# A depthwise convolution and two MLPs on one core: another order for the weight decoding, for the rounding passes and for the half-row copies

## The chip, the core and the metric

The program runs on one core of one Trainium2 chip. The metric is device time in microseconds (us), from the launch of the program to its end. The kernel before took 2457.29 us (median of three runs, 2455.79 to 2460.45).

## The reference

```python
# x (4, 4096, 192); weight (8, 7); w_in (192, 2048) and w_out (2048, 192), twice, both in float64
w = softmax(weight, axis=-1)                         # 7 taps for each of 8 heads of 24 channels
x = causal depthwise convolution of x with w         # 16384 tokens x 192 channels
h = x @ moe_w_in;   x = (h * cos(h)) @ moe_w_out     # first MLP
h = x @ moe2_w_in;  g = where(h > 0, h, exp(min(h, 0)) - 1)
out = g @ moe2_w_out                                 # second MLP
```

The results are float32. TensorE takes a rounded 32-bit type, so each operand is split into a high part and a low part (value minus high part), and each product is made of three: low x high, high x low, high x high.

## The kernel before

**Blocks, passes, steps.** The 16384 tokens are 32 blocks of 512. Four blocks make a group, and a group is done in two passes of 32 steps: first MLP (m = 1) for its four blocks, then second MLP (m = 2) for the same four. There are eight groups, so 512 steps, 8 to a block. A step handles two of the 16 slices of 128 hidden units.

**One step.** `emit_A(s)` issues 18 matmuls in 9 pairs into two PSUM tiles, `u` and `v` (192 channels are 128 + 64, so every product is cut into 64-row pieces that run in pairs). `emit_B(s - 2)` issues the 20 matmuls (10 pairs) of the second product for the step two earlier. Between them lie, for each of the two slices: `act1` (ScalarE, reads PSUM), for m = 1 also `mid` (VectorE), `act2` (ScalarE: Sin or Exp), `g` (VectorE, reads PSUM again and so frees it), then `emit_hi` (ScalarE rounds g to `gh`) and `emit_lo` (GpSimd subtracts: `gl`). `hi` and `lo` of step s are issued in step s + 1, and B uses them in step s + 2. In B, pairs 1 to 3 read `gh` of the first slice, 4 and 5 its `gl`, 6 to 8 `gh` of the second and 9 and 10 its `gl`.

**Order.** The order on every engine is the order in which `step` writes the instructions; engines run their own list in order and wait on semaphores. In a step of the kernel before, ScalarE has: act1 of both slices, then hi, act2, hi, act2.

**End of a block.** In the step with j = 1 of the next block `evac` copies two accumulators out (ScalarE, `e`, L574), adds the two others to them (VectorE, L577), and queues `sums`: a ScalarE copy of a half (L585), a GpSimd add (L587), and then for m = 1 the split of the result for the second MLP (ScalarE `zh`, `zc`, GpSimd `zl`, `zc`) or for m = 2 two VectorE transposes and six output DMAs. `sums` and the splits are generators in a list of chores; two chore calls are made in a step, the first in the list goes first.

**Operands of the next block.** `split` (m = 1) rounds the convolved block and fills the four doubled tiles `sh`, `sl`, `ch`, `cl` by eight half-row DMAs; `double_z` does so for m = 2. They are begun AHEAD steps before the block. All those DMAs, the x loads and the output go through SP's queue, which waits in order.

**Convolution.** The first four blocks are convolved with matrix products; later ones on VectorE (a transpose and seven passes, L347 to L360), two calls of the generator `cq` a step while m = 2 runs. When the convolution of a block begins, the x load of a later block is issued (`load_a`, L252).

**Weights.** They are float64 in DRAM and are decoded by integer operations, in 24 pieces of up to 256 columns for each MLP: part one (ScalarE 1 or 2, VectorE 3 or 4 instructions, L178 to L184), a GpSimd add (L186), a ScalarE rounding (L218, L239), a GpSimd subtraction (L220, L241). `prepare` keeps up to four pieces in flight and moves each one stage a call; `need` calls it until the weights of a step are there. The second MLP's raw pieces use three buffers and may start when block 3 is convolved.

Of the kernel before, what the change touches and what calls it, by code (L numbers as in the profile page):

```python
# [17 lines left out]
P = 128  # L18
N = 512
# [7 lines left out]
EARLY = 4  # L27
CALLS = 4
FLIGHT = 4
PRE1, PRE2 = 10, 3  # L30
W = 256
ROWS = 4
AHEAD = 5
# [4 lines left out]
def conv_then_two_mlps(ctx, tc, x, weight, w_in1, w_out1, w_in2, w_out2, out):  # L38
# [36 lines left out]
    stage = brief.enter_context(tc.tile_pool(name="stage", bufs=FLIGHT))  # L75
# [85 lines left out]

    def decode(m, load, n):

        raw = raw_tile(m)[:, 0:n]
        load(raw)
        yield  # L170
        lo, hi = raw[..., 0], raw[..., 1]
        w = stage.tile([P, W], F32, tag="w", name="w")[:, 0:n]
        bits = w.bitcast(I32)

        both = two if m == 1 else stage.tile([P, 2, W], F32, tag="t", name="t", bufs=1)
        size, low = both[:, 0, 0:n], both[:, 1, 0:n]
        if m == 1:
            nc.scalar.activation(out=size, in_=f32(hi), func=AF.Abs)  # L178
        else:
            nc.vector.tensor_scalar(out=size.bitcast(I32), in0=hi, scalar1=~SIGN, scalar2=0, op0=ALU.bitwise_and, op1=ALU.bitwise_or)  # L180
        nc.scalar.activation(out=low, in_=lo.bitcast(U32), func=AF.Copy, scale=2.0 ** -51, bias=2.0)
        nc.vector.tensor_scalar(out=size, in0=size, scalar1=2.0 ** -15, scalar2=2.0 ** 17 - 2.0 ** 13, op0=ALU.max, op1=ALU.min)
        nc.vector.tensor_scalar(out=bits, in0=size.bitcast(I32), scalar1=3, scalar2=0, op0=ALU.logical_shift_left, op1=ALU.bitwise_or)
        nc.vector.scalar_tensor_tensor(out=lo, in0=hi, scalar=SIGN, in1=low.bitcast(I32), op0=ALU.bitwise_and, op1=ALU.bitwise_or)  # L184
        yield
        nc.gpsimd.tensor_tensor(out=bits, in0=bits, in1=lo, op=ALU.add)  # L186
        yield w

    def prep_w_in(m, kind, j, n, queue):
# [29 lines left out]
        yield  # L219
# [3 lines left out]
    def prep_w_out(m, part, f0, f1, queue):  # L223
# [16 lines left out]
        yield  # L240
# [158 lines left out]
    def conv_by_products(what, b):  # L399


        xT = xTs.pop((what, b))
        if what == "a":
            o = ps_h.tile([P, N], F32, tag="u0", name="y")
        else:
            o = yb.pop() if yb else ps_a.tile([P, N], F32, tag=ACC[3], name="y")
        taps = lower_taps if what == "a" else upper_taps
        for k, w in enumerate(taps):
            nc.tensor.matmul(o, lhsT=w, rhs=xT[0:w.shape[0], k * Q:k * Q + N], start=k == 0, stop=k == len(taps) - 1)
            yield  # L410
        if what == "a" and b > 1:
# [25 lines left out]
    def doubles():  # L437
        return [dup.tile([P, N], F32R, tag=n, name=n) for n in ("sh", "sl", "ch", "cl")]
# [9 lines left out]
    def upper_split(b):  # L448

        yc = ys.pop(("c", b))  # L450
        ready_x[b] = d = doubles()
        nc.scalar.activation(out=d[2], in_=yc, func=AF.Copy)
        nc.vector.tensor_tensor(out=d[3], in0=yc, in1=f32(d[2]), op=ALU.subtract)

    def split(b):
        if ("c", b) in ys and b >= 2:
            yield from split_pair(b)
        ya = ys.pop(("a", b))
        xh = xt.tile([P, N], F32R, tag="xh", name="xh")
        xl = xt.tile([P, N], F32R, tag="xl", name="xl")  # L460
        nc.scalar.activation(out=xh, in_=ya, func=AF.Copy)
        yield
        nc.vector.tensor_tensor(out=xl, in0=ya, in1=f32(xh), op=ALU.subtract)
        split_done.add(b)
        yield
# [149 lines left out]
    def prepare():  # L615


        q = deque()
        for m in (1, 2):
            order = []  # L620
            for j in range(0, NP, 2):
                order += [("o", j, 1), ("c", j, 2), ("os", 2 * j, 4), ("oh", 2 * j, 2)]
                order += [("o", j + 1, 1), ("oh", 2 * j + 2, 2)]
            if m == 1:
                order[0:2] = [(0, 0, 1), (1, 0, 1), ("c", 0, 1), ("o", 1, 1), ("c", 1, 1)]
                order.remove(("o", 1, 1))
                order.insert(3, ("o", 1, 1))
            for kind, f0, n in order:
                queue = nc.scalar if len(q) < 2 else nc.sync
                if kind in ("os", "oh"):  # L630
                    g = prep_w_out(m, int(kind == "os"), f0, f0 + n, queue)
                else:
                    g = prep_w_in(m, kind, f0, n, queue)
                q.append(((kind, m, f0 + n), g))
        loaded, flight = deque(), deque()
        while len(loaded) < limit[1]:
            next(q[0][1])
            loaded.append(q.popleft())
        yield
        while q or loaded or flight:  # L640
            while q and len(loaded) + len(flight) < limit[q[0][0][1]] and (q[0][0][1] == 1 or ROWS - 1 in conved):
                next(q[0][1])
                loaded.append(q.popleft())
            if loaded and len(flight) < lanes[0]:
                flight.append(loaded.popleft())
            for it in list(flight):
                try:
                    next(it[1])
                except StopIteration:
                    flight.remove(it)  # L650
                    kind, m, at = it[0]
                    for k in ((0, 1) if kind == "o" else (kind,)):
                        ready[k, m] = at
            yield
        prepared.add(True)

    ready, prepared, banks = {}, set(), []
    limit, lanes = {1: PRE1, 2: PRE2}, [3]

    def need(m, at, *kinds):  # L660
        while any(ready.get((k, m), 0) < at for k in kinds):
            next(prep)

    prep = prepare()

    def convs():
# [10 lines left out]
        lower()  # L677
# [34 lines left out]
    begin_at = {max(s - AHEAD, 0): (m, b) for (m, b), s in first.items() if (m, b) != (1, 0)}  # L712
# [9 lines left out]
    def step(s):  # L722
# [11 lines left out]
        for q in now:  # L734
            emit_act1(q)
        for q in now:
            emit_mid(q)
# [4 lines left out]
        if 0 <= s - LAG < total:  # L742
# [3 lines left out]
            if j == NP - 1:  # L746
                finish = evac(m, b)
        for i in (0, 1):
            if calls > i:
                next(prep, None)  # L750
# [3 lines left out]
            if now:  # L754
                emit_act2(now[i])
            next(finish, None)
            if now:
                emit_g(now[i])
            busy = chore()
            if s < NP:  # L760
                for _ in range(EARLY // 2):
                    next(cq, None)
            elif len(conved) < GROUP or s >= total or steps[s][0] == 2:
                next(cq, None)
        for _ in range(calls - 2):
            next(prep, None)
# [8 lines left out]
    with tc.manual_schedule():  # L775
# [4 lines left out]
        next(prep)  # L780
# [4 lines left out]
        next(prep)  # L785
        next(prep)
        upper()
        n = 0
        while 0 not in conved:
            next(cq)  # L790
            n += 1
            if n in (5, 7, 9):
                next(prep)
        lanes[0] = FLIGHT
        for i, _ in enumerate(split(0)):
            if i == 1:
                upper_split(0)
# [33 lines left out]
```

## Time and profile before

| | |
|---|---|
| median of three runs | 2457.29 us |
| profiled execution: time / span | 2456.48 us / 2454.8 us |
| PE (matmul) busy | 2342.7 us, 95% |
| ScalarE, VectorE, GpSimd busy | 76%, 66%, 65% |
| mean granted TensorE clock | 0.982 |
| DMA | 112.14 MB, mean 46 GB/s |

The page's slices show PE at 99 to 100% from about the seventh slice on and lower before it: the first 300 us are another regime than the rest. PE is the engine that is nearest to its limit, so the question for every stretch is how much longer it is than the matmuls in it need, and which wait makes it so. A span of PE is modelled; where a stretch is measured below it is by the start times of the first matmul of B in a step.

### The profile page before, as it was taken

What the parts mean: (1) busy time and instruction counts of PE and PEld (TensorE: products, weight loads), DVE (VectorE), ACT (ScalarE), POOL (GpSimd) and SP (SyncE); (2) the same over time, 40 slices, a digit from 0 to 9 for tenths busy, and PEclk for the clock granted to TensorE, in tenths of its full rate; (3) what the DMA queues carried; (4) which work ended last, traced back from release to release, by engine and by line L of the source; (5) the groups of instructions that cost most, each with busy time, mean ns of one, the idle gap of its engine ahead of it and who ended that gap; (6) DMA issues with size and microseconds to landing.
All of it is one profiled execution on the core that took longest, in us unless ns stands there. A gap on an engine that the chain in (4) does not pass through costs nothing. (4 is left out here: it accounts for less than half of the span.)

```text
span 2454.8 us, 51057 instructions
## 1 busy us (share of the span) xinstructions
PE 2342.7 (95%) x19614; PEld 1896.1 (77%) x19614; DVE 1612.3 (66%) x2314; ACT 1860.3 (76%) x3544; POOL 1607.1 (65%) x1273
## 2 busy tenths in 40 slices
PE   7898699999999999999999999999999999999998
PEld 4576578887778877887877877788777887788886
DVE  5578687766756686666766667566776667666533
ACT  5576567887778877787777877778777887788876
POOL 5576656676666766576666676567666666667765
PEclk8999899999999999999999999999999999999999
DMA  5012223111311122212221212211132113112011
GB/s 152 18 40 69 67 51 71 34 44 30 60 37 36 36 55 41 54 29 48 43 47 38 53 30 53 43 42 36 36 60 46 26 36 60 31 42 53 19 36 26
DMA packets 279781, 112.14 MB, mean 46 GB/s; under 512 B 231920, under 2 KB 246512, under 8 KB 279536
## 3 DMA queue, kind: packets, MB, share of 16 engines
q1 hardware_dynamic: 279216, 108.62, 20.6%
q8 instruction: 153, 2.51, 0.4%
q14 instruction: 92, 0.75, 0.1%
q10 hardware_dynamic: 320, 0.26, 0.0%
HBM read 30.18 MB, written 12.58 MB: 17 GB/s over the span
## 5 line engine op out<-in xcount | busy, mean ns | idle before, releaser
L551 POOL TENSOR_TENSOR gl<-w,gh 128x512 fp32r<-128x512 f32 x1024 | 1359.1, 1340 | 797.5 <-ACT gh L546 481.4
L546 ACT ACTIVATE gh<-w 128x512 fp32r<-128x512 f32 x1024 | 645.9, 631 | 11.7 <-DVE w L540 8.0
L566 PE MATMUL b<-gh,wo_hl 64*128 64x512 f32 x2048 | 636.2, 391 | 10.4 <-DVE e L577 10.4
L566 PE MATMUL a<-gh,wo_hl 64*128 64x512 f32 x2048 | 638.8, 391 | 5.5 <-ACT gh L546 5.5
L566 PE MATMUL a<-gl,wo_hl 64*128 64x512 f32 x1024 | 409.1, 399 | 20.8 <-POOL gl L551 19.7
L540 DVE SCALAR_TENSOR_TENSOR w<-w,u 128x512 f32<-128x512 f32 x256 | 175.5, 686 | 381.5 <-ACT w L532 378.5
L566 PEld LDWEIGHTS a<-gh,wo_hl 64*128 64x128 f32 x2048 | 381.2, 186 | 57.6 <-ACT gh L546 6.0
L566 PEld LDWEIGHTS b<-gh,wo_hl 64*128 64x128 f32 x2048 | 379.4, 186 | 40.7 <-DVE e L577 18.5
L507 PE MATMUL u<-ch,wi_c 64*128 64x512 f32 x1024 | 401.9, 392 | 6.5 <-DMA ch<-ch 5.3
L566 PE MATMUL b<-gl,wo_hl 64*128 64x512 f32 x1024 | 406.3, 397 | 0.0
L507 PE MATMUL u<-sh,wi_o 64*128 64x512 f32 x1024 | 401.4, 392 | 1.6 <-DMA sh<-xh 1.6
L507 PE MATMUL v<-ch,wi_c 64*128 64x512 f32 x1024 | 400.9, 392 | 1.8 <-DMA ch<-ch 1.1
L507 PE MATMUL v<-sh,wi_o 64*128 64x512 f32 x1024 | 401.3, 392 | 0.0
L566 PE MATMUL b<-gh,wo_s 64*128 64x512 f32 x1024 | 400.0, 391 | 0.0
L566 PE MATMUL a<-gh,wo_s 64*128 64x512 f32 x1024 | 398.4, 389 | 0.0
L566 PE MATMUL a<-gl,wo_s 64*128 64x512 f32 x1024 | 397.8, 388 | 0.0
L566 PE MATMUL b<-gl,wo_s 64*128 64x512 f32 x1024 | 397.4, 388 | 0.0
L517 ACT ACTIVATE w<-u 128x512 f32<-128x512 f32 x256 | 152.6, 596 | 249.5 <-PE v L507 116.8
L515 ACT ACTIVATE w<-u 128x512 int32<-128x512 f32 x256 | 152.5, 596 | 235.0 <-PE v L507 94.4
L530 ACT ACTIVATE w<-w 128x512 f32<-128x512 f32 x512 | 321.6, 628 | 5.1 <-DVE w L524 4.9
L532 ACT ACTIVATE w<-w 128x512 f32<-128x512 f32 x512 | 321.9, 629 | 0.1
L524 DVE SCALAR_TENSOR_TENSOR w<-u,w 128x512 f32<-128x512 f32 x256 | 176.6, 690 | 217.3 <-ACT w L515 217.1
(128 smaller groups left out, 7117.6 us busy)
## 6 DMA issues: line engine op xcount, KB each, us to landing
out_dram<-e SPq DMA_DIRECT2D x192, 64.0 KB, 1.9
xa<-in_x_dram SPq DMA_DIRECT2D x112, 88.0 KB, 2.7
sh<-xh SPq DMA_DIRECT2D x64, 128.0 KB, 2.3
sl<-xl SPq DMA_DIRECT2D x64, 128.0 KB, 2.3
sh<-zh SPq DMA_DIRECT2D x64, 128.0 KB, 2.4
sl<-zl SPq DMA_DIRECT2D x64, 128.0 KB, 2.3
ch<-zc SPq DMA_DIRECT2D x64, 128.0 KB, 2.3
cl<-zc SPq DMA_DIRECT2D x64, 128.0 KB, 2.3
```

What stands on the lines that cost most here:

```text
L507: nc.tensor.matmul(u[i], lhsT=at, rhs=x[k + h][p], start=n == 0, stop=n == len(ops) - 1)
L515: nc.scalar.activation(out=w.bitcast(I32), in_=u, func=AF.Copy, bias=0.25)
L517: nc.scalar.activation(out=w, in_=u, func=AF.Relu, scale=-1.0)
L524: nc.vector.scalar_tensor_tensor(out=w, in0=u, scalar=0.25, in1=w.bitcast(I32), op0=ALU.add, op1=ALU.subtract)
L530: nc.scalar.activation(out=w, in_=w, func=AF.Sin, scale=6.283185)
L532: nc.scalar.activation(out=w, in_=w, func=AF.Exp, scale=-1.0)
L540: nc.vector.scalar_tensor_tensor(out=w, in0=w, scalar=-1.0, in1=u, op0=ALU.add, op1=ALU.max)
L546: nc.scalar.activation(out=gh, in_=wrk[s], func=AF.Copy)
L551: nc.gpsimd.tensor_tensor(out=gl, in0=wrk.pop(s), in1=f32(gs[s][0]), op=ALU.subtract)
L566: nc.tensor.matmul(a[o + i], lhsT=w[p, f, :], rhs=g[p], start=first, stop=final)
```

## The change

It has four parts.

- *Weight decoding.* `prepare` becomes `fetch` and `advance`. One call of `advance` does the rounding and subtraction of the piece before last, the add of the last one, and part one of a new piece. Three calls a step instead of four while the first MLP's weights are decoded, one a step afterwards. The order of pieces changes (`in_order`), a piece that was decoded twice is decoded once, and every second piece of the first MLP makes its absolute value on VectorE instead of ScalarE. The convolution's generator gets five calls a step until four blocks are convolved (before: four in the first eight steps, then two).
- *Rounding.* `hi` of the first slice comes first in a step, `hi` of the second in the middle. For m = 1: hi, act1, act1, hi, act2, act2; for m = 2: hi, act1, act2, hi, act1, act2. All of `evac` stands in the first half of a step.
- *Copies.* In `split`, each copy is issued right behind its source, `ch` and `cl` first.
- *AHEAD* is 6 instead of 5; block 1's convolved rows are copied from PSUM to SBUF; `lower()` is moved ahead of the first step.

```diff
-EARLY = 4
-CALLS = 4
-FLIGHT = 4
-PRE1, PRE2 = 10, 3
+EARLY = 5
+CALLS = 3
+RAW1, RAW2 = 10, 3
-AHEAD = 5
+AHEAD = 6
...
-        if m == 1:
+        turn[0] += 1
+        if m == 1 and turn[0] % 2:
             nc.scalar.activation(out=size, in_=f32(hi), func=AF.Abs)
...
     def split(b):
         if ("c", b) in ys and b >= 2:
             yield from split_pair(b)
+        sh, sl, ch, cl = doubles(("sh", "sl")) + ready_x.pop(b) if b < 2 else doubles()
+        if b >= 2:
+            p = half[b % 2]
+            both_halves(ch, pair["h"][p])
+            both_halves(cl, pair["l"][p])
...
         nc.scalar.activation(out=xh, in_=ya, func=AF.Copy)
+        swap(sh, xh)
         yield
         nc.vector.tensor_tensor(out=xl, in0=ya, in1=f32(xh), op=ALU.subtract)
+        swap(sl, xl)
         split_done.add(b)
-        yield
-        sh, sl, ch, cl = ready_x.pop(b) if b < 2 else doubles()
-        swap(sh, xh)
-        swap(sl, xl)
-        if b >= 2:
-            p = half[b % 2]
-            both_halves(ch, pair["h"][p])
-            both_halves(cl, pair["l"][p])
...
+    def fetch():
+        while todo and len(loaded) + len(begun) < raws[todo[0][1]] and (todo[0][1] == 1 or ROWS - 1 in conved):
+            next(todo[0][3])
+            loaded.append(todo.popleft())
+
+    def advance(new=True):
+        if added:
+            kind, m, at, g = added.popleft()
+            next(g)
+            for k in ((0, 1) if kind == "o" else (kind,)):
+                ready[k, m] = at
+        if begun:
+            next(begun[0][3])
+            added.append(begun.popleft())
+        if new and loaded:
+            next(loaded[0][3])
+            begun.append(loaded.popleft())
+        fetch()
...
-        for q in now:
-            emit_act1(q)
-        for q in now:
-            emit_mid(q)
...
+        first_mlp = now and steps[s][0] == 1
         for i in (0, 1):
-            if calls > i:
-                next(prep, None)
             if old:
                 emit_hi(old[i])
                 emit_lo(old[i])
-            if now:
+            if first_mlp and i == 0:
+                for q in now:
+                    emit_act1(q)
+                    emit_mid(q)
+            elif now and not first_mlp:
+                emit_act1(now[i])
                 emit_act2(now[i])
-            next(finish, None)
-            if now:
                 emit_g(now[i])
-            busy = chore()
-            if s < NP:
-                for _ in range(EARLY // 2):
-                    next(cq, None)
-            elif len(conved) < GROUP or s >= total or steps[s][0] == 2:
+            for _ in finish:
+                pass
+            if calls > i:
+                advance()
+            if first_mlp and i == 1:
+                for q in now:
+                    emit_act2(q)
+                    emit_g(q)
+            chore()
+            if len(conved) >= GROUP and (s >= total or steps[s][0] == 2):
                 next(cq, None)
```

In the order of the built programs (line numbers differ by one or two between them) this shows as follows. First ScalarE at a block's end in the first MLP, before:

```order
L546 ACTIVATE gh<-w 128x512
L530 ACTIVATE w<-w 128x512
L574 ACTIVATE e<-a_6108 128x512
L574 ACTIVATE e<-a_6110 128x512
L546 ACTIVATE gh<-w 128x512
L530 ACTIVATE w<-w 128x512
L585 ACTIVATE e<-e 64x512
L515 ACTIVATE w<-u 128x512
```

The same place now:

```order
L545 ACTIVATE gh<-w 128x512
L514 ACTIVATE w<-u 128x512
L514 ACTIVATE w<-v 128x512
L573 ACTIVATE e<-a_6096 128x512
L573 ACTIVATE e<-a_6098 128x512
L584 ACTIVATE e<-e 64x512
L545 ACTIVATE gh<-w 128x512
L529 ACTIVATE w<-w 128x512 x2
```

The copy of a half (L585, now L584), which stood behind the second rounding of `gh`, now stands ahead of it.

Next SP's queue where a second-MLP pass ends and the next group's first block gets its operands, before:

```order
L605 DMA out_dram<-e 32x16x32 x6
L252 DMA xa<-in_x_dram 32x22x32 x4
L442 DMA sh<-xh 64x512 x2
L442 DMA sl<-xl 64x512 x2
L446 DMA ch<-ch 64x512 x2
L446 DMA cl<-cl 64x512 x2
```

And now:

```order
L604 DMA out_dram<-e 32x16x32 x6
L446 DMA ch<-ch 64x512 x2
L446 DMA cl<-cl 64x512 x2
L442 DMA sh<-xh 64x512 x2
L442 DMA sl<-xl 64x512 x2
L252 DMA xa<-in_x_dram 32x22x32 x4
```

The x load, which was ahead of the eight copies, is behind them, and the `c` copies come first.

Last GpSimd in the first pass of group 0, where pieces of the second MLP's weights (adds L186, subtractions L220 and L241) stand among the `gl` of the steps, before:

```order
L241 TENSOR_TENSOR wo_hl<-w,wo_hl 128x256
L551 TENSOR_TENSOR gl<-w,gh 128x512 x2
L186 TENSOR_TENSOR w<-w,raw 128x256
L551 TENSOR_TENSOR gl<-w,gh 128x512 x2
L186 TENSOR_TENSOR w<-w,raw 128x256
L551 TENSOR_TENSOR gl<-w,gh 128x512 x2
L220 TENSOR_TENSOR wi_o<-w,wi_o 128x256
L186 TENSOR_TENSOR w<-w,raw 128x256
```

And now:

```order
L550 TENSOR_TENSOR gl<-w,gh 128x512 x2
L221 TENSOR_TENSOR wi_o<-w,wi_o 128x256
L188 TENSOR_TENSOR w<-w,raw 128x256
L550 TENSOR_TENSOR gl<-w,gh 128x512 x2
L221 TENSOR_TENSOR wi_o<-w,wi_o 128x256
L188 TENSOR_TENSOR w<-w,raw 128x256
L550 TENSOR_TENSOR gl<-w,gh 128x512 x2
L221 TENSOR_TENSOR wi_c<-w,wi_c 128x256
```

Before, 14 of the 24 pieces are added up to step 33 and the other ten in steps 34 to 39; now one piece is added in every step from 10 to 33, and it stands between the two `gl` of its step.

## Rows read from the trace of the kernel before

**Rows 1.** Page, part 1: busy us (share of the span) xinstructions of each engine.
```profile
PE 2342.7 (95%) x19614; PEld 1896.1 (77%) x19614; DVE 1612.3 (66%) x2314; ACT 1860.3 (76%) x3544; POOL 1607.1 (65%) x1273
```

**Rows 2.** B's matmuls (L566, 20 a step) by stretch: length, busy (count), clock, DMA.
```profile
46.70:126.00 79.30, 21.21 (x160) 0.91 0.11 30
126.00:255.20 129.20, 65.88 (x480) 0.97 0.20 53
255.20:319.20 64.00, 22.61 (x160) 0.84 0.28 65
...
434.50:574.30 139.80, 80.06 (x640) 1.00 0.15 34
574.30:725.00 150.70, 86.06 (x640) 0.98 0.25 49
```

**Rows 3.** The same, for eight steps each of passes of the second MLP.
```profile
1444.50:1482.30 37.80, 20.80 (x160) 1.00 0.24 48
1482.30:1518.80 36.50, 21.62 (x160) 1.00 0.32 61
...
1555.40:1595.20 39.80, 21.08 (x160) 0.96 0.24 47
2137.00:2171.80 34.80, 20.00 (x160) 1.00 0.20 43
```

**Rows 4.** Timeline of TensorE, SP's queue and ScalarE (start us, us): a group's first block.
```profile
1581.43 0.50 PE L507 MATMUL u<-ch,wi_c 64*128 64x512 f32 x1 [0.92 <-DMA ch<-ch]
...
1573.48 2.00 SPq L252 DMA_DIRECT2D xa<-in_x_dram  x4
...
1579.08 1.24 SPq L446 DMA_DIRECT2D ch<-ch  x2
...
1568.32 0.62 ACT L461 ACTIVATE xh<-y 128x512 fp32r<-128x512 f32 x1
```

**Rows 5.** Waits of 255.2 to 319.2 us: who for whom, total us, times, longest.
```profile
PE u L507 <- POOL wi_o L220: 18.8, 3, 10.1
```

**Rows 6.** Timeline of TensorE, ScalarE, VectorE, GpSimd: a block's end, first MLP.
```profile
1630.11 0.39 PE L566 MATMUL a<-gh,wo_hl 64*128 64x512 f32 x1
...
1631.92 0.39 PE L566 MATMUL a<-gl,wo_hl 64*128 64x512 f32 x1
...
1628.07 1.09 ACT L574 ACTIVATE e<-a 128x512 f32<-128x512 f32 x2
1629.03 0.65 ACT L546 ACTIVATE gh<-w 128x512 fp32r<-128x512 f32 x1
...
1630.22 0.63 ACT L585 ACTIVATE e<-e 64x512 f32<-64x512 f32 x1
1630.76 0.58 ACT L515 ACTIVATE w<-u 128x512 int32<-128x512 f32 x1
...
1628.82 1.28 DVE L577 SCALAR_TENSOR_TENSOR e<-b,e 128x512 f32<-128x512 f32 x2
...
1629.81 1.30 POOL L551 TENSOR_TENSOR gl<-w,gh 128x512 fp32r<-128x512 f32 x1 [0.72 <-ACT gh L546]
```

**Rows 7.** A piece of weights: VectorE and GpSimd timeline; GpSimd groups (busy, mean ns).
```profile
198.36 0.29 DVE L180 TENSOR_SCALAR t<-raw 128x256 int32<-128x256 int32 x1 [5.77 <-DMA raw<-in_moe_w_in_dram]
...
186.51 1.27 DVE L182 TENSOR_SCALAR t<-t 128x256 f32<-128x256 f32 x1
...
186.27 2.66 POOL L551 TENSOR_TENSOR gl<-w,gh 128x512 fp32r<-128x512 f32 x2
...
L186 POOL TENSOR_TENSOR w<-w,raw 128x256 int32<-128x256 int32 x24 | 19.0, 791 | 8.0 <-DVE raw L184 7.9
...
L241 POOL TENSOR_TENSOR wo_hl<-w,wo_hl 128x256 fp32r<-128x256 f32 x8 | 6.0, 756 | 0.0
```

**Rows 8.** VectorE and GpSimd timeline: a convolution pass beside three `gl`.
```profile
945.58 4.29 DVE L360 SCALAR_TENSOR_TENSOR y<-xT,wch,y 128x512 f32<-128x512 f32 x1
...
945.56 3.76 POOL L551 TENSOR_TENSOR gl<-w,gh 128x512 fp32r<-128x512 f32 x3
```

More of the change, by code (lines that the diff above doesn't have):

```diff
@@ L160, in raw_tile @@
         return t.rearrange("p (n two) -> p n two", two=2)
+    turn = [0]
     def decode(m, load, n):
@@ L410, in conv_by_products @@
             yield
-        if what == "a" and b > 1:
+        if what == "a":
             y = y_tile(what, b)
@@ L435, in conv_then_two_mlps, with doubles @@
     ready_x = {}
-    def doubles():
-        return [dup.tile([P, N], F32R, tag=n, name=n) for n in ("sh", "sl", "ch", "cl")]
+    def doubles(tags=("sh", "sl", "ch", "cl")):
+        return [dup.tile([P, N], F32R, tag=n, name=n) for n in tags]
     def swap(out, own):
@@ L450, in upper_split @@
         yc = ys.pop(("c", b))
-        ready_x[b] = d = doubles()
-        nc.scalar.activation(out=d[2], in_=yc, func=AF.Copy)
-        nc.vector.tensor_tensor(out=d[3], in0=yc, in1=f32(d[2]), op=ALU.subtract)
+        ready_x[b] = d = doubles(("ch", "cl"))
+        nc.scalar.activation(out=d[0], in_=yc, func=AF.Copy)
+        nc.vector.tensor_tensor(out=d[1], in0=yc, in1=f32(d[0]), op=ALU.subtract)
     def split(b):
@@ L612, in sums, with in_order @@
         yield
-    def prepare():
-        q = deque()
-        for m in (1, 2):
[L620 to L629, printed above, removed]
+    def in_order(m):
+        order = []
+        for j in range(0, NP, 2):
+            order += [("o", j, 1), ("c", j, 2), ("os", 2 * (j - 2), 4), ("oh", 2 * (j - 2), 2)]
+            order += [("o", j + 1, 1), ("oh", 2 * (j - 1), 2)]
+        order += [("os", NF - 4, 4), ("oh", NF - 4, 2), ("oh", NF - 2, 2)]
+        order = [o for o in order if o[1] >= 0]
+        if m == 1:
+            order[0:3] = [(0, 0, 1), (1, 0, 1), ("c", 0, 1), ("o", 1, 1), ("c", 1, 1)]
+        return order
@@ L630, in prepare, with pieces @@
+    def pieces():
+        for m in (1, 2):
+            for n, (kind, f0, c) in enumerate(in_order(m)):
+                queue = nc.scalar if m == 1 and n < 2 else nc.sync
                 if kind in ("os", "oh"):
-                    g = prep_w_out(m, int(kind == "os"), f0, f0 + n, queue)
+                    g = prep_w_out(m, int(kind == "os"), f0, f0 + c, queue)
                 else:
-                    g = prep_w_in(m, kind, f0, n, queue)
-                q.append(((kind, m, f0 + n), g))
@@ L635, in prepare @@
[L635 to L654, printed above, removed]
@@ L655, in prepare @@
-        prepared.add(True)
+                    g = prep_w_in(m, kind, f0, c, queue)
+                yield kind, m, f0 + c, g
+    todo = deque(pieces())
+    loaded, begun, added = deque(), deque(), deque()
+    raws = {1: RAW1, 2: RAW2}
+    def fetch():
[15 more added lines that the diff above has]
+        fetch()
+        if not (todo or loaded or begun or added):
+            prepared.add(True)
@@ L711, in conv_then_two_mlps @@
             first[m, b] = s
-    begin_at = {max(s - AHEAD, 0): (m, b) for (m, b), s in first.items() if (m, b) != (1, 0)}
+    begin_at = {max(s - AHEAD, EARLY): (m, b) for (m, b), s in first.items() if (m, b) != (1, 0)}
     chores = deque()
@@ L753, in step @@
                 emit_lo(old[i])
-            if now:
+            if first_mlp and i == 0:
[4 more added lines that the diff above has]
+                emit_act1(now[i])
                 emit_act2(now[i])
-            next(finish, None)
-            if now:
                 emit_g(now[i])
-            busy = chore()
-            if s < NP:
-                for _ in range(EARLY // 2):
-                    next(cq, None)
-            elif len(conved) < GROUP or s >= total or steps[s][0] == 2:
+            for _ in finish:
+                pass
+            if calls > i:
+                advance()
+            if first_mlp and i == 1:
[4 more added lines that the diff above has]
+            if len(conved) >= GROUP and (s >= total or steps[s][0] == 2):
                 next(cq, None)
         for _ in range(calls - 2):
-            next(prep, None)
+            advance()
+        if len(conved) < GROUP:
+            for _ in range(EARLY):
+                next(cq, None)
         if prepared and NP * GROUP <= s < 2 * NP * GROUP:
@@ L779, in conv_then_two_mlps @@
         load_pair(0, "ol")
-        next(prep)
+        fetch()
         nc.scalar.activation(out=spark, in_=ident[:, 0:H], func=AF.Exp)
@@ L784, in conv_then_two_mlps @@
         softmax_weights()
-        next(prep)
-        next(prep)
+        advance()
+        advance()
         upper()
@@ L791, in conv_then_two_mlps @@
             n += 1
[L792 to L797, printed above, removed]
+            if n in (6, 8):
+                advance(n == 6)
+        upper_split(0)
+        for _ in split(0):
+            pass
+        advance()
+        lower()
         need(1, 1, 0, 1, "c")
```

8 lines of the change are left out of this document (1 added, 7 removed).

## Prediction

> **What bounds the kernel now.** I read the page first, then B's matmuls by stretch, then the waits and the timelines where a stretch is too long. PE is busy for 95% of the span [rows 1], so what can be won or lost is the time by which a stretch exceeds its matmuls. Eight pairs of B take from 1630.11 to 1631.92 [rows 6], 0.226 us a pair; a step has 19 pairs, so 4.31 us. Against this [rows 2, 3]: a pass of 32 steps needs 137.9 us; first-MLP passes take 139.8 (2 us over), second-MLP passes 150.7 (13 over). In group 0, eight steps (34.5) take 79.3 at the start, 24 steps (103.4) take 129.2, and eight steps take 64.0 where the second MLP begins. Inside a second-MLP pass the quarters take 37.8, 36.5, about the same again, and 39.8: over by 3.3, 2.0, 2.0 and 5.3.
>
> The sum is made against the profiled execution, 2456.5 us (span 2454.8 and 1.7 around it); the median of the runs shown is 0.8 higher, so I add 0.8 at the end.
>
> **a) Copies with their source.** In the last quarter PE waits for `ch` [rows 4]: xh was made at 1568.3, but SP first waited to issue the x load (1573.48), then `sh` and `sl`, and `ch` only at 1579.08; PE got it at 1581.43. A last quarter in which no x load follows (the pass before the last group) takes 34.8 [rows 3]: 5.0 less, the halved clock after the wait included (0.96 against 1.00). In the new order the copies stand ahead of the x load, `ch` first, and are begun about a step and a half earlier; at most eight issues of 0.62 are ahead of any of them, so the last lands before the 8.6 us of two steps are over. Five crossings at 5.0, and the first group's, in the stretch before 434.5, at half of that: **-27 us**. Bounds: 0 if the copies stay late, -30.
>
> **b) Second MLP's weights.** In 255 to 319 us PE waits 18.8 us for GpSimd's `wi_o` pieces in three waits [rows 5], and starts anew at a low clock (0.84). Now the last piece is done by step 33. What stays is the change of pass (3.3 over, as in rows 3) and the convolution, which starts earlier by the same reason (I take 3): 34.5 + 6.5 = 41 for 64.0: **-23**. Bounds -28 (neither stays) and -15.
>
> **c) The same pieces inside the first pass.** Before, 14 pieces stand in these 24 steps, 25.8 us over, one wait of VectorE for a late raw piece (5.77, rows 7) among it. Now it is 24 pieces, one in each step, and the order closes a loop: `hi` of the first slice now precedes act1 on ScalarE, and needs g; g stands on VectorE behind part one of the piece; part one has to get past GpSimd. Alone, part one's passes take 0.29 each; beside a `gl` one took 1.27, until that `gl` ended [rows 7]. GpSimd's work in that place is `gl` 1.30 [rows 6], subtraction 0.76, add 0.79, `gl` 1.30: 4.1 us, begun 0.7 after g's end (`hi`, 0.65). Then two of part one's passes (0.29 and about 0.4) and g (0.64, as in the two of 1.28, rows 6): 0.7 + 4.1 + 0.7 + 0.64 = 6.2 a step; 6.85 if all four passes come after the last `gl`. I take 6.5, nearer to the row of 1.27: 24 x 6.5 + 3 for block ends = 159 for 129.2: **+30**. Bounds: without any waiting between the two engines the loop is `hi` and act1 (1.2), two mids (1.2), part one (1.3) and g (0.64), 4.4, so 24 x 4.4 + 6 = 112, -17; with all of it 24 x 6.85 + 6 = 170, +41.
>
> The Trainium skill has a rule for this, "SBUF — State Buffer", section "Who interferes with whom": a VectorE instruction with two SBUF inputs, or in a two-port mode, and a GpSimd instruction that reads SBUF exclude each other for a whole instruction, whoever issues first. The 1.27 beside 0.29 agrees. By it no VectorE pass waits for more than one GpSimd instruction, 1.3 us; but one convolution pass took 4.29 beside three `gl` of 3.76 together [rows 8], so the trace does not hold to that. With the rule at its word, the term e below would be 7 less.
>
> **d) First steps.** Up to 126 us no engine is full: VectorE, ScalarE and GpSimd each work little over half the time in a stretch of 79.3 for eight steps. The three stages no longer wait for one another inside a call, one piece of 25 is no longer done twice, and B of step 0 needs fewer pieces. From above, the engines' own work: GpSimd three pieces of 1.55 and two `gl`, 7.2 a step, 58 in all: -21. From below, VectorE's part one of the third piece and the convolution calls may now stand ahead of the next mid: +6. The nearest row is the 79.3 itself; I take a third of the way, **-8**. The copy of block 1, the earlier `lower()` and the absolute values moved to VectorE are in this.
>
> **e) Block ends.** Here the new order costs. At a block's end ScalarE copies two accumulators at 1628.07, VectorE adds from 1628.82 to 1630.10, and the copy of a half follows at 1630.22 [rows 6]. Before, the second `hi` (1629.03) was ahead of it, and its `gl` ended at 1631.1, in time for pair 9 of B at 1631.92. Now `hi` comes behind the copy, at 1630.76, ends at 1631.40, its `gl` runs to 1632.8: PE waits 0.95. Behind that, GpSimd's list in a first-MLP pass has eight operations of 1.26 in a row (gl, add, gl, gl, zl, gl, zc, gl); the last is now needed before it is done, by about 0.45. So 1.4 an end and 0.95 at the first end of a pass: 3 x 1.4 + 0.95 = 5.2 over, for 2.0 now. As the slots are tight I take 5.6: 7 passes (groups 1 to 7) x 3.6 = **+25**. Bounds +13 (first wait alone) and +42 (PE waits again for g).
>
> In second-MLP passes the quarters are now over by 3.3, 2.0, 2.0 and (without a) 0.3, 7.6 together. The first wait of 0.95 comes here too. Then, in two of the four ends, a convolution pass is pending on VectorE while GpSimd has gl, add, gl, gl; it gets in after one (second wait 0.95) or after three [rows 8] (2.2). I take 2.5 for each end, 3.4 for the change of pass, 1.0 for the last: 9.4, +1.8 x 6 passes, less 2 as their starts have more slack, and +2 in group 7, which has no convolution: **+11**. Bounds -7 and +24.
>
> Within a block nothing changes: ScalarE's passes follow each other by about 0.5 us [rows 6], six take 3.1 of 4.31 in either order, and the earlier `gl` only adds slack. That cover is gone at block ends alone, which is e.
>
> **Sum.** 2456.5 - 27 - 23 + 30 - 8 + 25 + 11 = 2464.5; with 0.8, **2465 us**.
>
> **Rivals.**
> *The pipeline pays (faster).* If part one slips between GpSimd's operations, the steps with a piece cost about 5.7, c is +10, and d comes out at the engines' own work, -21: 2465 - 20 - 13 = 2432. For it: VectorE passes of 0.29 are short, and the first MLP's pieces work in PSUM. Against it: the 1.27 row, and the loop over `hi`. It decides from a step of about 6.0 downwards.
> *GpSimd starves VectorE (much slower).* If passes wait for three operations as in rows 8 wherever GpSimd has a queue, c is +41, and e +42 and +24: 2465 + 11 + 17 + 13 = 2506. For it: the new order gives GpSimd longer queues at block ends. Against: of the convolution passes only a few at block ends show it.
> *The copies stay late.* If something else in SP's queue (raw pieces, outputs) is ahead, a is 0: 2492. Against it stands the order itself.
>
> **Chances.** My forecast 0.45 (its own range 2453 to 2480), pipeline pays 0.34, starving 0.16, copies late 0.05. The two large cases of both signs give 2425 to 2500 for 8 in 10. About 0.2% is what a measurement of this kernel can tell from no change, here 2452 to 2462; the forecast's lower edge and the pipeline case's upper one put 0.14 there, 0.38 below it and 0.48 above.
>
> **What would show it.** Right: no wait of PE for `ch` at the groups' crossings; PE without the 10 us waits at the second MLP's start; B of steps 8 to 32 in about 159 us; at each block end ScalarE's `gh` about 1.7 us later than now and PE waiting for `gl` about 1 us; first-MLP passes near 143.5 us, second-MLP passes near 147 to 148. Wrong: first-MLP passes still at 139.8 (then the half copy does not hold `gh` back in time that matters), steps with a piece below 6 us, or the start to 126 us shortened by more than 15.

## The result, and the profile after

The changed kernel takes 2473.7 us (median of four runs, 2472.95 to 2475.08) where the kernel before, run beside it, takes 2458.87 (2455.79 to 2462.28): a ratio of 1.0061, 95% interval 1.0043 to 1.0078. It is slower by 15 us, 0.4 to 0.8%. The forecast was 2465, slower by 8, with 2425 to 2500 as its range. In the profiled execution the span is 2471.2 for 2454.8.

Part 1 of the page after the change (busy us, share of the span, instructions), to be laid beside [rows 1]:

```profile
PE 2349.8 (95%) x19614; PEld 1955.0 (79%) x19614; DVE 1696.9 (69%) x2324; ACT 1926.3 (78%) x3529; POOL 1587.4 (64%) x1271
```

The same number of matmuls. VectorE is busy for 85 us more, although it has only ten instructions more: its passes have become longer, not more. Where the time went shows in B's matmuls (now L565) by the stretches of [rows 2], cut at the first B of steps 0, 8, 32 and 40, and then the first pass of group 1, the second, and a later first pass:

```profile
47.40:127.80 80.40, 20.46 (x160) 16.49 (x161) 0.87 0.12 34
127.80:280.70 152.90, 72.36 (x481) 49.27 (x480) 0.94 0.21 58
280.70:317.90 37.20, 22.14 (x160) 17.26 (x160) 0.97 0.42 75
435.10:579.70 144.60, 81.37 (x640) 60.35 (x641) 1.00 0.15 33
579.70:727.00 147.30, 83.84 (x641) 66.75 (x641) 1.00 0.25 50
...
1600.20:1743.60 143.40, 80.77 (x642) 61.98 (x642) 1.00 0.15 34
```

(The first number after the stretch is its length; the clock is the third from the end.) From step 0 to 8: 80.4 for 79.3; 8 to 32: 152.9 for 129.2; 32 to 40: 37.2 for 64.0; 40 to 64: 117.2 for 115.3. After that seven first-MLP passes are 27 us longer together (143.4 each for 139.8, 144.7 in group 1), six second-MLP passes 13 shorter (147.6 each for 149.8 in the mean), and the last pass is 2 longer. With B starting 0.6 later the whole comes to 16.4, the difference of the spans.

**Copies.** SP's queue for the same first block of a group as in [rows 4], and PE's first matmul that reads `ch`:

```profile
1574.30 1.28 SPq L446 DMA_DIRECT2D ch<-ch  x2
...
1580.65 1.10 SPq L442 DMA_DIRECT2D sl<-xl  x2
1581.85 2.30 SPq L252 DMA_DIRECT2D xa<-in_x_dram  x4
...
1590.19 0.39 PE L506 MATMUL u<-ch,wi_c 64*128 64x512 f32 x1
```

The copies into all four tiles are issued ahead of the x load, the last by 1581.75. The matmuls of the new block begin at 1589.5, eight microseconds later, and the first that reads `ch` starts without a wait. The last quarter of the second-MLP pass takes 35.5 for 39.8 [rows 3], at a clock of 1.00 for 0.96.

**A block's end.** The place of [rows 6], now with the order ScalarE (copies of two accumulators, half copy, `hi`), GpSimd, TensorE:

```profile
1633.51 1.09 ACT L573 ACTIVATE e<-a 128x512 f32<-128x512 f32 x2 [0.89 <-PE b L565]
1635.46 0.63 ACT L584 ACTIVATE e<-e 64x512 f32<-64x512 f32 x1 [0.86 <-DVE e L576]
1636.10 0.63 ACT L545 ACTIVATE gh<-w 128x512 fp32r<-128x512 f32 x1
...
1636.87 1.29 POOL L550 TENSOR_TENSOR gl<-w,gh 128x512 fp32r<-128x512 f32 x1 [4.65 <-ACT gh L545]
...
1638.21 0.50 PE L565 MATMUL a<-gl,wo_hl 64*128 64x512 f32 x1 [0.45 <-POOL gl L550]
```

GpSimd has been idle for 4.65 us when `hi` is done at last, its `gl` ends at 1638.16, and PE starts 0.05 later. By the starts of B that step takes 5.27 for 4.31 (the idle time of 0.45 in the row counts from a modelled end), and the one two steps on 4.89, at each of three ends in a pass; at the start of a pass there is the first wait alone.

**A step with a piece of weights**, between steps 8 and 32: VectorE from one g to the next, then GpSimd, then ScalarE's `hi`.

```profile
169.76 0.69 DVE L523 SCALAR_TENSOR_TENSOR w<-u,w 128x512 f32<-128x512 f32 x1 [0.65 <-ACT w L514]
...
170.96 0.53 DVE L182 TENSOR_SCALAR t<-raw 128x256 int32<-128x256 int32 x1
171.52 0.72 DVE L184 TENSOR_SCALAR t<-t 128x256 f32<-128x256 f32 x1
172.28 1.26 DVE L185 TENSOR_SCALAR w<-t 128x256 int32<-128x256 int32 x1
173.46 0.41 DVE L186 SCALAR_TENSOR_TENSOR raw<-raw,t 128x256 int32<-128x256 int32 x1
173.80 0.68 DVE L537 TENSOR_TENSOR w<-u,w 128x512 f32<-128x512 f32 x1
...
169.32 1.29 POOL L550 TENSOR_TENSOR gl<-w,gh 128x512 fp32r<-128x512 f32 x1 [1.89 <-ACT gh L545]
170.60 0.74 POOL L241 TENSOR_TENSOR wo_s<-w,wo_s 128x256 fp32r<-128x256 f32 x1
171.30 0.80 POOL L188 TENSOR_TENSOR w<-w,raw 128x256 int32<-128x256 int32 x1
172.06 1.34 POOL L550 TENSOR_TENSOR gl<-w,gh 128x512 fp32r<-128x512 f32 x1
...
168.61 0.63 ACT L545 ACTIVATE gh<-w 128x512 fp32r<-128x512 f32 x1 [2.17 <-DVE w L537]
174.57 0.63 ACT L545 ACTIVATE gh<-w 128x512 fp32r<-128x512 f32 x1 [2.17 <-DVE w L537]
```

This is the loop: `hi` at 168.61 needs g of the step before; its `gl` and GpSimd's next three operations run to 173.40; L185 ends with the last of them, L186 (0.41) and g follow, and the next `hi` starts at 174.57, 5.96 later. ScalarE is idle for 2.17 of that. Three of part one's passes end where a GpSimd operation ends, 0.14 behind it: L182 (0.53) with the subtraction, L184 (0.72) with the add, L185 (1.26) with the second `gl`. Such a pass takes 0.29 alone [rows 7]. Ten of the 24 steps are like this one; those at block ends take 6.6 to 9.5. There a pass can wait longer: in two of them L185 waits over three GpSimd operations (an add, a `gl` and a `zl`):

```profile
184.46 3.19 DVE L185 TENSOR_SCALAR w<-t 128x256 int32<-128x256 int32 x1
```

### The profile page after: what moved, and what is told of

Same layout as the page of the kernel before. It is cut to its first block, busy times and chain, and to the rows that moved or that the text cites. A ratio compares the mean times of both kernels' runs of the same rounds, so it can differ in the third digit from the quotient of the medians.

```text
span 2471.2 us, 51323 instructions
## 1 busy us (share of the span) xinstructions
PE 2349.8 (95%) x19614; PEld 1955.0 (79%) x19614; DVE 1696.9 (69%) x2324; ACT 1926.3 (78%) x3529; POOL 1587.4 (64%) x1271
## 4 chain that ended last, share of the span: by engine, by line
PE 67%; DVE 12%; ACT 8%; issue 6%; POOL 5%; DMA 0%; SPq 0%; DVEq 0%; POOLq 0%; ACTq 0%
PE a L565 27%; PE u L506 24%; PE v L506 8%; PE b L565 8%; POOL gl L550 4%; ACT gh L545 2%; DVE y L360 2%; DVE e L576 2%; ACT e L584 2%; DVE w L539 2%; DVE w L523 1%; DVE w L185 1%; ACT e L573 1%; DVE w L537 1%; ACT w L516 1%
## 5 line engine op out<-in xcount | busy, mean ns | idle before, releaser
L565 PE MATMUL a<-gh,wo_hl 64*128 64x512 f32 x2048 | 638.7, 391 | 2.2 <-ACT gh L545 2.2
L565 PE MATMUL b<-gh,wo_hl 64*128 64x512 f32 x2048 | 636.4, 391 | 0.9 <-DVE e L576 0.9
L565 PE MATMUL a<-gl,wo_hl 64*128 64x512 f32 x1024 | 408.7, 399 | 46.5 <-POOL gl L550 45.2
L565 PEld LDWEIGHTS a<-gh,wo_hl 64*128 64x128 f32 x2048 | 374.3, 185 | 59.9 <-ACT gh L545 19.6
L565 PE MATMUL b<-gl,wo_hl 64*128 64x512 f32 x1024 | 407.7, 398 | 0.0
L565 PE MATMUL b<-gh,wo_s 64*128 64x512 f32 x1024 | 397.2, 388 | 0.0
L565 PE MATMUL a<-gh,wo_s 64*128 64x512 f32 x1024 | 396.9, 388 | 0.0
L565 PE MATMUL a<-gl,wo_s 64*128 64x512 f32 x1024 | 396.5, 387 | 0.0
L565 PE MATMUL b<-gl,wo_s 64*128 64x512 f32 x1024 | 395.9, 387 | 0.0
L565 PEld LDWEIGHTS b<-gh,wo_hl 64*128 64x128 f32 x2048 | 373.5, 185 | 18.8 <-DVE e L576 3.0
L360 DVE SCALAR_TENSOR_TENSOR y<-xT,wch,y 128x512 f32<-128x512 f32 x264 | 382.1, 1447 | 0.9
L531 ACT ACTIVATE w<-w 128x512 f32<-128x512 f32 x512 | 323.7, 632 | 16.1
L529 ACT ACTIVATE w<-w 128x512 f32<-128x512 f32 x512 | 294.7, 629 | 1.6 <-DVE w L523 1.5
L565 PEld LDWEIGHTS a<-gl,wo_hl 64*128 64x128 f32 x1024 | 189.0, 185 | 111.9 <-POOL gl L550 93.0
```

Of the source, the lines that this page charges most:

```text
L360: nc.vector.scalar_tensor_tensor(out=o, in0=i, scalar=w, in1=o, op0=ALU.mult, op1=ALU.add)
L529: nc.scalar.activation(out=w, in_=w, func=AF.Sin, scale=6.283185)
L531: nc.scalar.activation(out=w, in_=w, func=AF.Exp, scale=-1.0)
L565: nc.tensor.matmul(a[o + i], lhsT=w[p, f, :], rhs=g[p], start=first, stop=final)
```

## The experiments

Theory at the outset: two places of the new step order cost time (the half copy ahead of `hi` at block ends, and the loop through part one of a piece), the copies and the earlier second-MLP weights gain it. The rival for the block ends: GpSimd's list itself is too long there; for the loop: VectorE is simply starved by GpSimd, whatever the order. The first eight kernels have one time each, beside 2458.2 us (the first four) or 2459.8 (the next four) of the kernel before on the same chip. The kernel before ranges from 2455.79 to 2462.28 when it is repeated, so a few microseconds between two such times show nothing by themselves; the stretches in the traces decide then.

### Half copy later

```diff
-            for _ in finish:
-                pass
+            ended = [0 for _ in finish]
...
-            chore()
+            if not ended:
+                chore()
```

> The changed kernel with one edit: in the step in which evac runs, the chore of the first half is left out, so ScalarE's half copy of the block's end stands behind the second rounding of gh again. Theory (the copy waits for VectorE's two adds and holds back the second gh, hence gl): the wait of 0.95 us of PE at each block's end goes, and the second one of 0.58 in first-MLP passes with it, since GpSimd's row of operations moves back too. First-MLP passes 143.4 to about 140, second-MLP passes 147.6 to about 144, the whole about 2425 us. Rival 1 (the wait comes from the rounding's new place or from evac in one half): passes stay at 143.4 and 147.6, 2474 us. Rival 2 (half a wait: the chores only move it to the next step): passes 141.5 and 146, 2445 us.

Measured: **2395.45 us**, 78 less than the changed kernel and 63 less than the kernel before. ScalarE and GpSimd at the same block's end, and B's matmuls in a first and a second pass of this kernel:

```profile
1586.59 0.63 ACT L545 ACTIVATE gh<-w 128x512 fp32r<-128x512 f32 x1
...
1588.29 0.63 ACT L584 ACTIVATE e<-e 64x512 f32<-64x512 f32 x1
...
1587.35 1.30 POOL L550 TENSOR_TENSOR gl<-w,gh 128x512 fp32r<-128x512 f32 x1 [3.02 <-ACT gh L545]
```

```profile
429.90:567.70 137.80, 77.73 (x642) 59.93 (x641) 1.00 0.15 35
567.70:711.20 143.50, 84.45 (x640) 66.03 (x639) 1.00 0.26 51
```

`hi` now stands before the half copy, and its `gl` ends at 1588.65, ahead of PE's need for it at 1589.50. First-MLP passes take 137.8, what 32 steps of 4.31 need: the wait is gone, and also the 2 us a pass that the kernel before lost. So the place of the half copy carried the whole of the block ends' cost in the first MLP, 5.6 us a pass, and half of it in the second (9.8 to 5.1). The edit also puts the chores behind the copy half a step later, GpSimd's add among them; for the first wait the rows show that it was the copy, for the second this was not tried apart. GpSimd's list is not too long. The expectation was 30 too high, for the most part because it took the kernel before as the floor of the passes.

### Decoding behind g

```diff
-            if calls > i:
-                advance()
...
-        for _ in range(calls - 2):
+        for _ in range(calls):
             advance()
```

> The changed kernel with all calls of advance at the end of a step, behind g, instead of ahead of it. Theory (in steps with a piece g waits on VectorE behind part one, and the first rounding, and with it act1 of the next step, waits for g): 24 steps with one piece go from 152.9 us to about 130, and the first eight from 80.4 to about 68, since PE waits there for g too; later passes unchanged, 143.4 and 147.6; the whole about 2440. Rival (VectorE and GpSimd exclude each other, so their work adds up wherever it stands): 24 steps about 148, the first eight about 80, the whole about 2470.

Measured: **2489.91 us**, 16 slower than the changed kernel. The expectation fails. VectorE and GpSimd in a step with a piece, then all engines from step 8 to 32 (busy of PE, PEld, DVE, ACT, POOL):

```profile
173.00 1.27 DVE L185 TENSOR_SCALAR w<-t 128x256 int32<-128x256 int32 x1
174.19 1.51 DVE L186 SCALAR_TENSOR_TENSOR raw<-raw,t 128x256 int32<-128x256 int32 x1
...
172.77 2.65 POOL L550 TENSOR_TENSOR gl<-w,gh 128x512 fp32r<-128x512 f32 x2
```

```profile
129.40:294.30 164.90, 132.06 (x915) 98.89 (x911) 154.87 (x194) 102.49 (x209) 107.93 (x102) 0.91 0.20 53
```

Part one now runs beside the same four GpSimd operations: its first two passes end behind the subtraction and the add, and the last two wait out one `gl` each (1.27 and 1.51). VectorE is busy for 154.9 of 164.9 us and sets a step of 6.63. So taking part one out of the loop does not take it off the path: the price is that its passes stand beside GpSimd. In that the rival was right, though its figures were too low as well (148 us for the 24 steps, 2470 for the whole). The order of the change was the cheaper of the two.

### Copies alone, in the kernel before

```diff
-AHEAD = 5
+AHEAD = 6
...
+        if b >= 2:
+            sh, sl, ch, cl = doubles()
+            both_halves(ch, pair["h"][p])
+            both_halves(cl, pair["l"][p])
         nc.scalar.activation(out=xh, in_=ya, func=AF.Copy)
+        if b >= 2:
+            swap(sh, xh)
...
```

> The kernel before with one part of the change: from block 2 on, split issues each copy behind its source, ch and cl first, and blocks are begun six steps ahead (block 1 at the step of before). Theory (the x load ahead of the copies is what PE waits for): second-MLP passes of groups 1 to 5 from 150.7 to about 145.7, that of group 6 unchanged at 146.7, first-MLP passes unchanged at 139.8, the whole 27 us less, about 2431. Rival (PE waits there for the DMAs' own landing or for VectorE): passes stay at 150.7, 2458 us.

Measured: **2430.28 us**, 28 less than the kernel before. Last quarters of second-MLP passes are 4.35 a step, and first passes stay at 139.8. By the traces the span is 26 shorter: 22.4 of that is in the five passes that the theory names (4.3 to 5.0 each), and most of the rest is in steps 8 to 32, 123.5 for 129.2. The first eight steps take 81.8 for 79.3. The copies' term stands by itself in the passes; what the start gains or loses by it is less sure, as two profiles of one kernel further down differ there by 3 to 4 us.

### The old step order with the new pipeline

```diff
+        for q in now:
+            emit_act1(q)
+        for q in now:
+            emit_mid(q)
...
         for i in (0, 1):
+            if calls > i:
+                advance()
             if old:
                 emit_hi(old[i])
                 emit_lo(old[i])
-            if first_mlp and i == 0:
-                for q in now:
-                    emit_act1(q)
-                    emit_mid(q)
-            elif now and not first_mlp:
-                emit_act1(now[i])
+            if now:
                 emit_act2(now[i])
+            next(finish, None)
+            if now:
                 emit_g(now[i])
...
```

> The changed kernel with the step's order of before: act1 of both slices first, then rounding, act2, g, in each half; evac in two halves; advance first in each half as the decoding was before; three-stage pipeline, copies and AHEAD as changed. Theory (the rounding at even places costs, the rest gains): first-MLP passes back to 139.8, second-MLP passes 145.7 (150.7 without the 5.0 at the crossing), 24 steps with pieces 152.9 to about 135 because the loop over the rounding is open, first eight about 80; the whole about 2425. Rival (the rounding's place is neutral and the passes are longer for AHEAD or the copies): first-MLP passes stay at 143.4, 2465 or more.

Measured: **2412.66 us**. B's matmuls from step 0 to 8, 8 to 32, and in group 1's two passes:

```profile
48.50:120.50 72.00, 21.12 (x161) 16.58 (x161) 0.91 0.14 38
120.50:261.40 140.90, 66.93 (x481) 49.76 (x480) 0.96 0.23 63
414.00:553.40 139.40, 78.81 (x640) 59.60 (x639) 1.00 0.15 34
553.40:699.60 146.20, 84.26 (x642) 65.10 (x643) 1.00 0.25 51
```

Block ends are back at the old cost (2 over in a first pass). What was not expected is the start: 72.0 for 80.4. With the old order the new pipeline and what came with it do shorten the first eight steps, by 7.3 against [rows 2]; the new order of a step takes it all back. Here that order is the place of the rounding, of `evac` and of `advance` together; they were not tried one by one. The stretch from 8 to 32 is 12 shorter than in the changed kernel. The start scatters, but less than this: five traces with the new order in it take 80.4 to 83.1 us for the first eight steps, five with the new pipeline and the old order there 70.0 to 74.8.

### No convolution pass beside the add

On top of the half copy later:

```diff
         eng.tensor_tensor(out=e[2][lo], in0=e[2][lo], in1=e[3][lo], op=ALU.add)
-        yield
+        yield 2
...
-            if len(conved) >= GROUP and ...
+            did = None if ended else chore()
+            if did != 2 and len(conved) >= GROUP and ...
```

> The changed kernel with the half copy later, and besides no convolution step in the half step in which GpSimd gets its add of the two halves. In the kernel with the half copy later the second-MLP passes are still 5.1 us over, in two places of 1.7 (PE waits 1.40 us for VectorE's last pass of the activation) and at the change of pass. Theory: the convolution's pass that is given to VectorE in that half waits 3.86 us over the add and two subtractions, and the activation's pass waits behind it. Then the two places go, 3.4 us in each of 6 second-MLP passes: 2395 - 20 = 2375 us. Rival 1: the pass given in the next half meets the two subtractions instead and waits 2.6; PE still waits a little, 1 us saved in a pass: 2389. Rival 2: PE waits there for another reason, and nothing moves: 2395.

Measured: **2378.14 us**, 17 less; second-MLP passes 139.5 for 142.9. VectorE and GpSimd with the pass beside the add (the kernel with the half copy later), and then without it:

```profile
888.33 0.69 DVE L539 SCALAR_TENSOR_TENSOR w<-w,u 128x512 f32<-128x512 f32 x1 [1.37 <-ACT w L531]
888.93 3.86 DVE L360 SCALAR_TENSOR_TENSOR y<-xT,wch,y 128x512 f32<-128x512 f32 x1
892.72 0.67 DVE L539 SCALAR_TENSOR_TENSOR w<-w,v 128x512 f32<-128x512 f32 x1
...
888.45 1.28 POOL L586 TENSOR_TENSOR e<-e 64x512 f32<-64x512 f32 x1
889.70 2.54 POOL L550 TENSOR_TENSOR gl<-w,gh 128x512 fp32r<-128x512 f32 x2
```

```profile
887.34 0.69 DVE L539 SCALAR_TENSOR_TENSOR w<-w,u 128x512 f32<-128x512 f32 x1 [0.31 <-ACT w L531]
889.01 0.69 DVE L539 SCALAR_TENSOR_TENSOR w<-w,v 128x512 f32<-128x512 f32 x1 [0.98 <-ACT w L531]
```

The activation's pass for `v` starts 1.67 us after that for `u`, for 4.39 with the convolution pass between them. One of the two places is clean now; at the other a wait of PE of about 0.5 us for a `gl` is left.

### Old order while weights are decoded

On top of the half copy later: the step of the fourth experiment as long as `calls` is not 0, the new one afterwards.

> The changed kernel with the half copy later, but with the order of a step as it was before as long as weights are decoded (steps 0 to 33). Theory: in the changed order the hi of the first slice, the first passes of the activation, part one of the piece and g form one loop, 5.96 us a step from step 8 on, and it holds in the first eight steps too (80.4 us); in the old order the next hi need not wait for g behind part one, the first eight steps take 72.0 and the next 24 take 141, as in the kernel with the whole old order (261.4 - 48.5 = 212.9 for steps 0 to 32, against 236.6). Then about 22 us less than with the half copy later alone: 2374. Rival: what the stretch of decoding gains is lost where the order changes at step 33, or the half copy is what made it short: 2385 to 2395.

Measured: **2371.2 us**, 24 less than with the half copy later alone. B starts step 8 after 71.8 us and step 32 after another 140.8, and nothing is lost at the switch. With this the new order of a step is priced by place: it costs 24 us in the first 32 steps (236.6 for 212.6), and after them, with the half copy out of its way, it gains 1.9 us in each first pass and 2.9 in each second one (137.8 and 142.9 for the fourth experiment's 139.7 and 145.8).

### Absolute values on ScalarE

The changed kernel with one line:

```diff
-        if m == 1 and turn[0] % 2:
+        if m == 2 or turn[0] % 2:
```

> The changed kernel with one edit: the absolute values of the second MLP's pieces are taken on ScalarE, not on VectorE, one pass of 0.53 us less in VectorE's part one. Theory (the loop): a step with a piece is as long as hi, the first passes of the activation, part one and g, one after another; ScalarE is idle for 2.17 us of it. Then each of 24 steps is 0.5 shorter: 5.4 for 5.96, 2474 - 12 = 2462 us. Rival (GpSimd sets it): the passes left only wait for the same GpSimd operations to end, and part one still ends when it did: 2474, steps of 5.96.

Measured: **2466.89 us**, 7 less, which a single time hardly tells from scatter; the steps do. Those with a piece take 5.77 for 5.96: nearer to the rival. VectorE and GpSimd in such a step:

```profile
170.59 0.72 DVE L185 TENSOR_SCALAR w<-t 128x256 int32<-128x256 int32 x1
171.24 1.51 DVE L186 SCALAR_TENSOR_TENSOR raw<-raw,t 128x256 int32<-128x256 int32 x1
...
171.12 1.35 POOL L550 TENSOR_TENSOR gl<-w,gh 128x512 fp32r<-128x512 f32 x1
```

One pass less, and the last of the three that stay ends with the same `gl` (172.47) that ended L185 before. So most of the loop's length is GpSimd's four operations, and it gives only 0.19 of the 0.53. The stretch from 8 to 32 is 142.3 for 152.9, of which 24 x 0.19 explains 5; the rest is in steps at block ends and, with a granted clock of 1.00 for 0.94, was not taken apart. The first eight steps, which the edit does not touch, took 83.1 for 80.4, and steps 32 to 40 another 2.0 longer, so the whole gains less than the stretch.

### All three together

> The three edits together: half copy later with no convolution step beside the add, old order of the step while weights are decoded, absolute values of the second MLP's pieces on ScalarE. If each does what its theory says and the last is worth 5 us in the old order, where ScalarE has less room: 2395 - 20 - 22 - 5 = 2348 us. If the convolution's pass waits elsewhere and the absolute values bring nothing: 2374.

Measured: **2350.77 us**. Then the same kernel in rounds:

> The kernel with all three edits again, now timed against the kernel before in three rounds: 2351 us, ratio 0.956 (0.954 to 0.958). If its one run was a lucky one, up to 2360.

Measured: **2349.76 us** (2345.48 to 2351.75) against 2460.07 of the kernel before, a ratio of 0.9547, interval 0.9531 to 0.9563. All engines in its passes of the first and the second MLP:

```profile
682.60:820.40 137.80, 137.80 (x1220) 126.05 (x1218) 92.64 (x141) 116.27 (x216) 95.34 (x75) 1.00 0.15 35
820.40:959.90 139.50, 139.10 (x1219) 121.37 (x1217) 109.41 (x130) 117.85 (x211) 93.92 (x71) 1.00 0.28 56
```

PE shows no idle time in this first-MLP pass.

### Every absolute value on ScalarE

The same, with the first MLP's pieces too:

> The kernel with all three edits, and besides every absolute value on ScalarE, the first MLP's too, as in the kernel before. Theory: in the first eight steps ScalarE waits 7.3 us in eight waits for VectorE's absolute values (t L182), since both write one tile; without them the start is 3 to 6 us shorter, 2346 us. Rival: ScalarE is the later engine there, as its piece follows the activation, and one more pass of 0.4 in its chain makes the start 2 us longer: 2353.

Measured: **2346.29 us** (2344.71 to 2348.57), a ratio of 0.9538, interval 0.9524 to 0.9552. The start is 70.0 and the next stretch 131.9; the two profiles of the kernel with three edits had 74.8 and 131.6, 72.0 and 135.4. So the start is 2 to 5 us shorter, about as expected, but these two profiles of one kernel differ by 3 to 4 us in each stretch, and the intervals of the whole overlap: not settled.

## Why the prediction was right, and where it was not

The direction is right, and 2473.7 lies near the forecast of 2465. The step itself was 15 us (2458.87 to 2473.7) where 8 were forecast, so about half of it. Most terms hold one by one, but that the sum came so near is in part luck: b and c together came out 10 us lower than forecast and d 9 higher, and steps 40 to 64, the first group's second-MLP pass behind its change of pass, lost 1.9 where 2.5 were to be gained. No term covered the block ends in that stretch; with the half copy later it takes 108.5 for 117.1. Small slips in the working (19 pairs of 0.226 make 4.29, not 4.31; in b 3.3 and 3 were taken as 6.5; in d a third of 21 as 8) change none of this.

- **a, copies, -27:** right. Alone in the kernel before they bring 28, 22.4 of it at the five crossings for which 25 were forecast; in the changed kernel the last quarter before a crossing goes from 39.8 to 35.5. At the first group's crossing nothing is seen of the 2.5 (steps 40 to 64 take 115.6 for 115.3 with the copies alone).
- **b, second MLP's weights, -23:** measured -26.8 from step 32 to 40. PE's 18.8 us of waits for `wi_o` [rows 5] have no successor; what PE still waits for in that stretch is g, 0.6 us.
- **c, pieces in the first pass, +30:** measured +23.7. The loop is the one described, with 0.7 of `hi` and 4.1 of GpSimd's operations in it. I had counted two passes of part one behind the last `gl` and rounded up to 6.5; one comes behind it, and the step is 5.96. The steps at block ends are longer than the 3 us allowed for them, others a little shorter; the mean is 6.37. Half of the term is there in the old order too (129.2 to 140.9), half comes with the new order of a step (to 152.9).
- **d, first steps, -8:** this failed; measured +1.1. With the old order the rest of the change is worth -7.3 there, as forecast, but the term took a third of the way to the engines' own work and left out the loop of c. That loop holds in any step with pieces, and steps 0 to 7 have three each: as PE's waits show (before, then after, us in total, times, longest), those for GpSimd's pieces gave way to those for g, which come to 4.4 us before and 13.0 after.

```profile
PE u L507 <- POOL wi_o L220: 7.3, 3, 4.0
...
PE v L507 <- DVE w L538: 3.4, 2, 2.7
```

```profile
PE v L506 <- DVE w L537: 4.4, 1, 4.4
...
PE xps L310 <- DVE w L537: 3.4, 1, 3.4
```

- **e, block ends, +25 and +11:** right. First-MLP passes are 5.6 over (5.6 forecast, though the second wait is 0.6 for 0.45 and the 0.4 added for tight slots made up for it), second-MLP passes 9.8 (9.4 forecast). The first wait is 0.95 a step, the second at the two convolution ends 1.8 by the starts of B (6.1 for 4.31; 1.55 was taken), between the two cases. The convolution pass at one such end:

```profile
1493.33 3.85 DVE L360 SCALAR_TENSOR_TENSOR y<-xT,wch,y 128x512 f32<-128x512 f32 x1
```

  Here the rule of the Trainium skill weighed in the prediction ("SBUF — State Buffer", section "Who interferes with whom") would have given 0.95 for the second wait, some 10 us too little over six passes: the convolution pass waits for three GpSimd operations, 3.85 us, at two ends of a pass and for two, 2.61, at its start. In the step with a piece shown above the trace agrees with it: each pass waits for one GpSimd operation.

Of the rivals, the pipeline that pays needed steps below 6.0; they are at 5.96, yet the block ends in that stretch (mean step 6.37) and the lost start kept it away. A step below 6 was also named as a sign of being wrong; it was met by 0.04, while the stretch came out between the forecast's 159 and that rival's figure. Starving of VectorE over three or more operations shows in steps 8 to 32 of the change in three passes alone (3.63 and twice 3.19), at block ends, and in the convolution passes of e. The prediction named the half copy as what holds `gh` back. What it did not see is that most of its largest cost, 36 us of block ends, goes with that one place, and that the new order has a gain of its own under it, where it took the earlier `gl` for mere slack: 41 us between the fourth experiment (2412.66) and the sixth (2371.2), which differ only after the decoding.

## What to carry to other kernels

When an instruction is moved forward in a list, look at the rare steps in which something else is in the list ahead of it: an average step had slack, and four block ends in a pass paid for the move. Work out a term of one part of a change with the order that the other parts leave behind, not with the old one. And look at what GpSimd has queued where a short VectorE pass stands: in these traces the same pass took 0.29 us, about 1.3 or 3.2. What was not priced alone: block 1's copy, the earlier `lower()` and AHEAD without the copies.

## What was not expected of the hardware

One VectorE pass over 128x256 int32 (L185 of the changed kernel) has a mean of 1.27 us over the second MLP's 24 pieces. Four of the 24 took 0.29, eighteen 1.25 to 1.32, and two 3.19; each of these twenty ended 0.15 behind the end of a GpSimd subtraction. So the same pass was held up by one GpSimd operation in most steps and by three in two. A convolution pass of 128x512 next to an add and two subtractions waited for all three (3.86). In the steps with a piece that are shown a pass got in after each GpSimd operation; what makes the difference was not tried.
